# Sixteen products of the identity with itself on TensorE, ahead of the fourth unit of attention

## The chip, the cores and the metric

One Trainium2 chip, one of its cores. The metric is the device time of one execution in microseconds (us), and of several executions the median. TensorE (PE in the rows) multiplies matrices, VectorE (DVE) and ScalarE (ACT) work element by element, GpSimd (POOL) and SyncE (SP) here only fill the identity and start transfers.

## The reference

Attention in blocks of 64 over 576 positions, then two feed-forward layers over the 2304 tokens, all in 32-bit floats. Cut to what matters here:

```python
scores = scale * np.matmul(q, k.transpose(0, 1, 3, 2))          # 4 batches x 8 heads, 576 x 576
scores = np.where(block_i >= block_j, scores, -1000000000.0)
attn = np.exp(scores - np.max(scores, axis=-1, keepdims=True))
attn = attn / (np.sum(attn, axis=-1, keepdims=True) + 1e-09)
x = np.matmul(attn, v)                                           # -> 2304 tokens x 512
h = x @ w_in;  g = softplus(h);  x = g @ w_out                   # 512 -> 2048 -> 512
h = x @ w_in2; e = softmax(h) * h, normalised; out = e @ w_out2  # 512 -> 1024 -> 512
```

## The kernel before

The program is one list of tasks for five engines. Each task has an engine, a planned duration, a rank (lower goes first) and the tasks that it needs. A planner (`Plan.run`) plays the list through with the planned durations and, each time that an engine is free, takes the ready task of lowest rank; what comes out is a fixed order of instructions for each engine. On the chip every engine works through its order and waits at semaphores, so an instruction that isn't ready holds up all behind it.

The start is made of three kinds of work that share the engines. The first 256 positions of each pair of heads are handled by sixteen units `UnitA`: a load of q and k (`qkA`), a score product into a PSUM bank (`mm_qk`: four products, each of which the trace shows as two instructions), on VectorE a mask and two maxima (`mask`, `max`, `scale`), on ScalarE the exponentials (`exp`), on VectorE the division (`norm`), on TensorE six transposes (`tr`), a copy to SBUF (`psA`), the product with v (`pv`), and the result split in two into `xt`. The first four units use the banks `R`, `r`, `acc` and, for the fourth, the two banks `hp0` and `hp1` in which the first feed-forward layer later builds its hidden values. Beside them, `Piece` turns weights that come in by DMA (`raw`) into two parts each, on ScalarE (L273) and VectorE (L276 to L293). `Pair` is the feed-forward layer itself: products `hp<-xt,w`, softplus, and products into `acc`.

The identity matrix `ident`, 128x128, is filled by GpSimd in the first task of all (`open_a`, here the task `t_open`). Transposes use it as one operand. A product of 32-bit floats on TensorE goes in two passes (the two instructions above).

The later stages (the remaining 320 positions, the second feed-forward layer) are not touched by the change.

Of the kernel before, what the change touches and what calls it, by code (L numbers as in the profile page):

```python
# [51 lines left out]
class Plan:  # L52
# [8 lines left out]
    def add(self, eng, dur, rank, fn, deps=(), lat=None):  # L61
        t = _Task()
        t.key = key_of(fn)

        t.alts = dict(eng) if isinstance(eng, dict) else {eng: dur}
        name, i = t.group = self.group
        t.local = rank
        t.rank = rank + RANK[name][0] + RANK[name][1] * i + OFF.get(t.key, 0.0) + OFF.get(t.key + "@" + name, 0.0)
        t.eng, t.fn, t.n, t.done = None if len(t.alts) > 1 else eng, fn, len(self.tasks), False
        t.lat = (self.LAT + (120.0 if eng == "PE" else 0.0)) if lat is None else lat  # L70
        t.users, t.left, t.ready = [], 0, 0.0
        for d in deps:
            if d is not None:
                d.users.append(t)
                t.left += 1
        self.tasks.append(t)
        return t
# [5 lines left out]
    def chain(self, eng, rank, steps, deps):  # L83
        for dur, fn in steps:
            t = self.add(dur if isinstance(dur, dict) else eng, dur, rank, fn, deps)
            deps = [t]
        return t
# [83 lines left out]
def key_of(fn):  # L171
    while isinstance(fn, partial):
        fn = fn.func
    return ".".join(fn.__qualname__.split(".")[-2:])
# [6 lines left out]
def dve_ns(n, per=1.04):  # L181
    return 70.0 + per * n
# [6 lines left out]
def dma_ns(nbytes, n=1):  # L189
    return max(50.0 + nbytes / 360.0, 550.0 * n)  # L190
# [3 lines left out]
def body(ctx: ExitStack, tc: tile.TileContext, qk, qkA, vP, vA, w1, w2, u1, u2, gln, out):  # L194
    nc = tc.nc
    PE, ACT, DVE, POOL, SP = nc.tensor, nc.scalar, nc.vector, nc.gpsimd, nc.sync
    plan = Plan()
    XTB, LAG = 3, 2
    add, chain = plan.add, plan.chain
    DMA_LAT = 1700.0  # L200

    def mm(out, lhsT, rhs, start, stop):
        PE.matmul(out, lhsT, rhs, start=start, stop=stop, skip_group_check=True)  # L203
# [9 lines left out]
    def at_of(lst, i):  # L213
        return lst[i] if 0 <= i < len(lst) else None
# [25 lines left out]
    ident = pw.tile([128, 128], F32, name="ident")  # L240
    gcol = pw.tile([128, 48], F32, name="gcol")[:, 0:8]
    acc = qsh.tile([128, 2, 512], F32, name="acc")
    hps = [qsh.tile([128, 2, CT], F32, name=f"hp{i}") for i in range(2)]
# [3 lines left out]
    class Piece:  # L247
# [3 lines left out]
        def plan(self, prev, rank, get, nr, na, first=(), free=()):  # L251
            oldr, olda = at_of(prev, len(prev) - nr), at_of(prev, len(prev) - na)
            self.get, self.n = get, len(prev)
            dep = ([prev[-1].t_load] if prev else []) + ([oldr.t_bits] if oldr else []) + list(first)
            self.t_load = add("SP", dma_ns(524288), rank, self.load, dep, DMA_LAT)
            t = add("ACT", 570, rank, self.abs, [self.t_load] + ([olda.t_lo] if olda else []))
            self.t_bits = chain("DVE", rank, ((335, self.bits0), (602, self.bits1), (602, self.bits2)), [t])
            if self.g is None:
                self.t_hi = add({"ACT": 520, "DVE": 335}, None, rank, self.do_hi, [self.t_bits] + list(free))
                self.t_lo = add("DVE", 610, rank, self.do_lo, [self.t_hi])  # L260
            else:
                self.t_hi = add("ACT", 520, rank, self.do_hi_g, [self.t_bits] + list(free))
                self.t_lo = add("DVE", 602, rank, self.do_lo_g, [self.t_hi])
            prev.append(self)
# [54 lines left out]
    def xfree(c):  # L319

        return [t for u in pairs if u.c == c - XTB for t in (u.t_a0, u.t_a1)]
# [142 lines left out]
    class UnitA:  # L464
# [6 lines left out]
        def plan(self, prev, rank, opened):  # L471
            n = self.n = len(prev)
            p1, p2 = at_of(prev, n - 1), at_of(prev, n - 2)

            def g(u, *names):
                return [getattr(u, x) for x in names] if u else []


            self.bank = ("R", "r", "acc", "hp")[n] if n < 4 else "r" if n in (8, 9, 10, 11) else ("r", "R")[n % 2]
            free = [u.t_xl for u in prev if u.bank == self.bank][-1:]  # L480
            if n >= 12 and self.bank == "R":
                free += evacs[1]
            self.t_qk = add("SP", dma_ns(262144), rank - 2, self.load_qk, [opened] + g(p1, "t_v") + g(at_of(prev, n - 3), "t_mqk"), DMA_LAT)
            self.t_v = add("SP", dma_ns(131072), rank - 2, self.load_v, [opened, self.t_qk] + g(p2, "t_pv"), DMA_LAT)
            self.t_mqk = add("PE", 760, rank, self.mm_qk, [self.t_qk] + free)
            t = chain("DVE", rank, ((200, self.mask), (330, partial(self.max, 0)), (600, partial(self.max, 1)), (70, self.scale)), [self.t_mqk])
            t = add("ACT", 1580, rank, self.exp, [t] + g(p2, "t_tr"))
            t = chain("DVE", rank, ((72, self.den0), (90, self.den1), (918, self.norm)), [t])
            self.t_tr = add("PE", 650, rank, self.tr, [t])
            self.t_cp = add({"ACT": 708, "DVE": 870}, None, rank, self.copy, [self.t_tr] + g(p1, "t_pv"))  # L490
            self.t_pv = add("PE", 718, rank, self.pv, [self.t_cp, self.t_v])
            self.t_xh = add({"ACT": 264, "DVE": 335}, None, rank, self.x_hi, [self.t_pv] + xfree(self.b))
            self.t_xl = add("DVE", dve_ns(NA), rank, self.x_lo, [self.t_xh])
            xparts.setdefault(self.b, []).append(self.t_xl)
            prev.append(self)
# [229 lines left out]

    NR, NCA = 3, 4
    t_open = add("POOL", 500, 0.0, open_a, ())

    pairs, unitsA, unitsC = [], [], []
    pieces, w1ready, w2ready = [], {}, {}  # L730
# [278 lines left out]
```

## Time and profile before

| | |
|---|---|
| three runs | 818.89, 815.85, 818.53 us; median 818.53 us |
| profiled execution, its own time | 818.25 us |
| span in the profile, first to last instruction | 816.5 us |
| TensorE busy | 790.5 us (97% of the span) |
| VectorE busy | 546.0 us (67%) |
| ScalarE busy | 391.9 us (48%) |
| mean granted TensorE clock | 0.991 |

The time of an execution is 1.75 us more than its span: what lies before the first and after the last instruction. Granted clock 1.00 stands for TensorE's full 2.4 GHz, 0.50 for 1.2 GHz. The busy shares are means over the whole span; the first 60 us look quite different from the rest, and the rows further down show them apart.

### The profile page before, as it was taken

Reading aid. Unit: us, or ns where it says so; the run is one execution under the profiler, and the core shown is the slowest. Engines: PE = TensorE matmul, PEld = TensorE weight load, DVE = VectorE, ACT = ScalarE, POOL = GpSimd, SP = SyncE. Lnnn points to the kernel's source line nnn. Section 1 sums busy time; section 2 is a strip of 40 time slices with the busy share of each in tenths; the row PEclk is TensorE's granted clock in tenths of the full one; section 3 lists DMA queues with packets and bytes.
Section 4 is the critical chain, followed back from the end, with each engine's and each line's share of the span. In section 5 each row is a group of like instructions: output and inputs, shape, how many; then the busy total and the mean of one; then the engine's idle time right before and its main releaser. Section 6 shows DMA issues by size and latency. Waiting matters only on the chain.

```text
span 816.5 us, 14229 instructions
## 1 busy us (share of the span) xinstructions
PE 790.5 (97%) x5656; PEld 684.6 (84%) x5656; DVE 546.0 (67%) x1273; ACT 391.9 (48%) x863; POOL 0.7 (0%) x6
## 2 busy tenths in 40 slices
PE   5689999999999999999999999999999999999998
PEld 3478889998888788888887889999988888888887
DVE  6989999575666665665565652776949576766661
ACT  5566775554555545455554543645623232322232
POOL 0000000000000000000000000000000000000000
PEclk9799999999999999999999999999999999999999
DMA  5636551202121112112211100326301111110001
GB/s 166 214 119 192 175 165 63 92 10 79 49 83 41 42 42 67 41 42 71 61 41 41 58 3 26 105 78 207 117 27 39 51 39 53 39 51 27 26 26 51
DMA packets 31201, 59.63 MB, mean 73 GB/s; under 512 B 2848, under 2 KB 14368, under 8 KB 31136
## 3 DMA queue, kind: packets, MB, share of 16 engines
q1 hardware_dynamic: 31136, 58.74, 22.5%
q8 instruction: 44, 0.72, 0.4%
q14 instruction: 21, 0.17, 0.1%
HBM read 49.29 MB, written 9.44 MB: 72 GB/s over the span
## 4 chain that ended last, share of the span: by engine, by line
PE 80%; DVE 13%; DMA 3%; ACT 2%; issue 2%; SPq 0%; ACTq 0%; DVEq 0%
PE hp L203 19%; PE acc L203 18%; PE op L203 12%; PE h L203 11%; PE S L203 6%; PE O L203 5%; PE T L437 4%; PE tp L905 2%; PE R L203 2%; DVE a L283 2%; DMA raw<-in_w_dram 2%; DVE a L279 1%; DVE t L641 1%; DVE gl L649 1%; PE r L203 1%
## 5 line engine op out<-in xcount | busy, mean ns | idle before, releaser
L203 PE MATMUL hp<-xt,w 128*128 128x256 f32 x1728 | 218.9, 281 | 1.1 <-DVE t L641 1.0
L203 PEld LDWEIGHTS hp<-xt,w 128*128 128x128 f32 x1728 | 205.9, 189 | 5.4 <-issue 3.4
L203 PE MATMUL acc<-gh,w 128*128 128x256 f32 x768 | 150.3, 286 | 0.0
L203 PEld LDWEIGHTS acc<-gh,w 128*128 128x128 f32 x768 | 122.4, 189 | 13.0 <-issue 12.5
L203 PE MATMUL acc<-gl,w 128*128 128x256 f32 x384 | 107.0, 279 | 0.6 <-DVE gl L649 0.6
L203 PE MATMUL op<-w,w2w 128*128 128x512 f32 (+1 forms) x456 | 102.3, 381 | 0.0
L203 PE MATMUL h<-u,w 128*128 128x512 f32 x432 | 100.9, 390 | 0.0
L203 PEld LDWEIGHTS h<-u,w 128*128 128x128 f32 x432 | 80.7, 188 | 16.5
L203 PEld LDWEIGHTS op<-w,w2w 128*128 128x128 f32 x456 | 81.5, 188 | 15.3
L632 ACT ACTIVATE t<-hp 128x512 f32<-128x512 f32 x72 | 42.9, 596 | 79.3 <-PE hp L203 74.5
L209 ACT ACTIVATE ps<-T 128x512 f32<-128x512 f32 (+1 forms) x77 | 42.7, 554 | 75.0 <-PE T L437 60.3
L203 PEld LDWEIGHTS acc<-gl,w 128*128 128x128 f32 x384 | 72.7, 189 | 0.8 <-DVE gl L649 0.8
L641 DVE SCALAR_TENSOR_TENSOR t<-hp,t 128x512 f32<-128x512 f32 x72 | 49.4, 686 | 26.4 <-ACT t L638 26.0
L416 ACT ACTIVATE eC<-S,mC 128x384 f32<-128x384 f32 (+2 forms) x80 | 51.7, 653 | 11.6 <-DVE mC L410 11.5
L406 DVE TENSOR_REDUCE mC<-S 128x2 f32<-128x768 f32 (+2 forms) x48 | 46.9, 976 | 7.9 <-PE S L203 7.2
L203 PE MATMUL S<-qkC 64*128 64x384 f32 (+2 forms) x192 | 51.9, 533 | 0.0
L649 DVE TENSOR_TENSOR gl<-t,gh 128x512 fp32r<-128x512 f32 x72 | 49.6, 689 | 2.8 <-ACT gh L209 1.5
L203 PE MATMUL acc<-gh,w2w 128*128 128x256 f32 x256 | 50.2, 285 | 0.9 <-DVE gh L211 0.7
L857 ACT ACTIVATE e<-h,mx 128x1024 f32<-128x1024 f32 x18 | 20.1, 1116 | 55.1 <-PE tp L905 48.6
L203 PEld LDWEIGHTS acc<-gh,w2w 128*128 128x128 f32 x256 | 40.5, 188 | 6.9 <-issue 5.5
L638 ACT ACTIVATE t<-t 128x512 f32<-128x512 f32 x72 | 45.4, 630 | 2.0
L635 ACT ACTIVATE t<-t 128x512 f32<-128x512 f32 x72 | 45.4, 631 | 1.1
(149 smaller groups left out, 1050.4 us busy)
## 6 DMA issues: line engine op xcount, KB each, us to landing
raw<-in_w_dram SPq DMA_DIRECT2D x32, 512.0 KB, 3.9
qkC<-in_qk_dram SPq DMA_DIRECT2D x16, 480.0 KB, 3.4
raw_u<-in_u_dram SPq DMA_DIRECT2D x11, 512.0 KB, 3.5
v<-in_vP_dram SPq DMA_DIRECT2D x16, 320.0 KB, 3.0
x2s<-stg SPq DMA_DIRECT2D x18, 256.0 KB, 2.2
xr<-x2s SPq DMA_DIRECT2D x18, 256.0 KB, 3.1
qkA<-in_qkA_dram SPq DMA_DIRECT2D x16, 256.0 KB, 3.3
out_dram<-ob SPq DMA_DIRECT2D x15, 256.0 KB, 2.0
```

The source lines that it names most:

```text
L203: PE.matmul(out, lhsT, rhs, start=start, stop=stop, skip_group_check=True)
L209: ACT.activation(out, a, AF.Copy)
L283: DVE.scalar_tensor_tensor(out=self.a, in0=self.raw[:, :, 0], scalar=29, in1=self.a, op0=ALU.logical_shift_right, op1=ALU.bitwise_or)
L406: DVE.tensor_reduce(out=self.m[:, 0:n], in_=self.scores(i), axis=AX.X, op=ALU.max, negate=True)
L416: ACT.activation(state["eC"][i][:, j, :], self.scores(i)[:, j, :], AF.Exp, scale=0.125, bias=m[:, j:j + 1], accum_out=den[:, j:j + 1])
L437: PE.transpose(T[:, 128 * k:128 * k + 128], e[:, 128 * k:128 * k + 128], ident)
L632: ACT.activation(self.t, self.hp, AF.Abs)
L635: ACT.activation(self.t, self.t, AF.Exp, scale=-1.0)
L638: ACT.activation(self.t, self.t, AF.Ln, bias=1.0)
L641: DVE.scalar_tensor_tensor(out=self.t, in0=self.hp, scalar=0.0, in1=self.t, op0=ALU.max, op1=ALU.add)
L649: DVE.tensor_sub(self.gl, self.t, self.gh)
L857: ACT.activation(self.e, self.hh, AF.Exp, bias=self.mx, accum_out=self.ss)
```

## The change

Sixteen tasks are added. Each is one product of the identity with itself, 128x128 by 128x128, written to the bank `hp1`. They need only `t_open`; their rank is 1,000,000 plus what the group adds, so the planner takes one only when no other task of TensorE is ready. The score product of the fourth unit, which takes `hp0` and `hp1`, is made to come after them. Nothing reads what they write.

```diff
@@ UnitA.plan
             if n >= 12 and self.bank == "R":
                 free += evacs[1]
+            if self.bank == "hp":
+                free += idle
@@ body
     t_open = add("POOL", 500, 0.0, open_a, ())
+
+    def idle_product():
+
+        mm(hps[1][:, 0, 0:128], ident, ident, True, True)
+
+
+    idle = [add("PE", 400, 1e6, idle_product, [t_open]) for i in range(16)]
```

On TensorE, at the very start of the program, the order of before is this. `R`, `r` and `acc` are the banks of the first three units; `qkA` is a unit's q and k, `eA_130` and `eA_131` are exponentials of the first two units; x2 means that a row stands for two products.

```order
L203 MATMUL R<-qkA 128x128 x2
L203 MATMUL R<-qkA 128x256 x2
L203 MATMUL r<-qkA 128x128 x2
L203 MATMUL r<-qkA 128x256 x2
L203 MATMUL acc<-qkA 128x128 x2
L203 MATMUL acc<-qkA 128x256 x2
L556 MATMUL R<-ident,eA_130 128x128 x6
L556 MATMUL r<-ident,eA_131 128x128 x6
```

And this is the order of the changed kernel at the same place (its line 558 is line 556 of before).

```order
L203 MATMUL hp_115<-ident 128x128 x7
L203 MATMUL R<-qkA 128x128 x2
L203 MATMUL R<-qkA 128x256 x2
L203 MATMUL hp_115<-ident 128x128
L203 MATMUL r<-qkA 128x128 x2
L203 MATMUL r<-qkA 128x256 x2
L203 MATMUL hp_115<-ident 128x128 x2
L203 MATMUL acc<-qkA 128x128 x2
L203 MATMUL acc<-qkA 128x256 x2
L203 MATMUL hp_115<-ident 128x128 x6
L558 MATMUL R<-ident,eA_130 128x128 x6
L558 MATMUL r<-ident,eA_131 128x128 x6
```

The sixteen products (`hp_115` is `hp1`) stand in four places: seven ahead of the first unit's scores, one and two ahead of the second's and the third's, and six between the third's scores and the first transposes. Behind that TensorE's order is unchanged. The first of the seven waits for GpSimd's identity; the first transpose no longer needs to.

VectorE, ScalarE, SyncE and GpSimd keep their orders word for word, and their waits too. What VectorE does at this start is this: mask, maxima and scaling (L523, L528, L531) of the three units, in turn, then the divisor of the first (L541, L544).

```order
L523 MEMSET R 64x4x64
L528 TENSOR_REDUCE mA<-R 128x2 x2
L523 MEMSET r 64x4x64
L531 TENSOR_SCALAR mA<-mA 128x4
L528 TENSOR_REDUCE mA<-r 128x2 x2
L523 MEMSET acc 64x4x64
L531 TENSOR_SCALAR mA<-mA 128x4
L528 TENSOR_REDUCE mA<-acc 128x2 x2
L541 TENSOR_SCALAR dA<-dA 128x4
```

Nothing moved there.

## Rows read from the trace of the kernel before

**Rows 1.** The page: span, engines' busy time, share and instructions.
```profile
span 816.5 us, 14229 instructions
PE 790.5 (97%) x5656; PEld 684.6 (84%) x5656; DVE 546.0 (67%) x1273; ACT 391.9 (48%) x863; POOL 0.7 (0%) x6
```

**Rows 2.** Windows: from:to, length, busy (instructions) by engine, granted clock, DMA share, GB/s.
```profile
0.00:9.81 9.81, 4.96 (x24) 2.80 (x24) 2.62 (x8) 2.99 (x9) 0.70 (x6) 1.00 0.75 256
9.81:41.40 31.59, 20.45 (x120) 14.87 (x121) 31.25 (x95) 20.59 (x62) 0.00 (x0) 0.84 0.51 166
60.00:140.00 80.00, 76.61 (x651) 72.22 (x651) 77.70 (x172) 54.07 (x115) 0.00 (x0) 1.00 0.47 152
140.00:800.00 660.00, 658.80 (x4656) 569.33 (x4655) 416.82 (x956) 299.38 (x643) 0.00 (x0) 1.00 0.18 55
```

**Rows 3.** Timeline, first 28 us, TensorE: start, length, work [idle before, releaser].
```profile
3.69 1.65 PE L203 MATMUL R<-qkA 64*128 64x128 f32 x8 [3.69 <-DMA qkA<-in_qkA_dram]
5.87 1.65 PE L203 MATMUL r<-qkA 64*128 64x128 f32 x8 [0.53 <-DMA qkA<-in_qkA_dram]
8.02 1.66 PE L203 MATMUL acc<-qkA 64*128 64x128 f32 x8 [0.49 <-DMA qkA<-in_qkA_dram]
...
11.96 1.69 PE L556 MATMUL R<-ident,eA 128*128 128x128 f32 x6 [2.29 <-ACT eA L537]
...
19.73 0.93 PE L203 MATMUL hp<-qkA 64*128 64x128 f32 x8 [0.17 <-DMA qkA<-in_qkA_dram]
...
27.62 1.65 PE L203 MATMUL R<-qkA 64*128 64x128 f32 x8 [3.77 <-DMA qkA<-in_qkA_dram]
```

**Rows 4.** Timeline of the first 10 us and of 41 to 43 us, VectorE.
```profile
5.47 0.27 DVE L523 MEMSET R<- 64x256 f32 x1 [5.47 <-PE R L203]
...
7.66 0.27 DVE L523 MEMSET r<- 64x256 f32 x1 [0.86 <-PE r L203]
...
9.81 0.27 DVE L523 MEMSET acc<- 64x256 f32 x1 [0.82 <-PE acc L203]
...
43.09 0.27 DVE L523 MEMSET r<- 64x256 f32 x1 [1.27 <-PE r L203]
```

**Rows 5.** Timeline of the first 11 us, GpSimd's last fill of the identity, and ScalarE.
```profile
1.00 0.29 POOL masks.py:199 TENSOR_SCALAR_AFFINE_SELECT ident<-ident 128x128 f32<-128x128 f32 x1
...
8.10 0.37 ACT L537 ACTIVATE eA<-R,mA 128x128 f32<-128x128 f32 x1 [6.09 <-DVE mA L531]
...
10.24 0.37 ACT L537 ACTIVATE eA<-r,mA 128x128 f32<-128x128 f32 x1 [0.42 <-DVE mA L531]
```

**Rows 6.** Timeline, TensorE: full 32-bit products (two), and what comes next.
```profile
202.72 1.19 PE L203 MATMUL S<-qkC 128*128 128x512 f32 x4
203.72 1.66 PE L203 MATMUL hp<-xt,w 128*128 128x256 f32 x12
```

**Rows 7.** Windows of one us: granted clock (before DMA share) where it changes.
```profile
28.00:29.00 1.00, 1.00 (x8) 0.55 (x6) 1.00 (x6) 1.00 (x7) 0.00 (x0) 0.50 0.76 311
...
33.00:34.00 1.00, 1.00 (x6) 0.79 (x6) 1.00 (x3) 0.33 (x2) 0.00 (x0) 0.76 0.02 7
...
37.00:38.00 1.00, 1.00 (x5) 1.00 (x6) 1.00 (x6) 0.33 (x1) 0.00 (x0) 0.50 1.02 369
...
40.00:41.00 1.00, 1.00 (x9) 1.00 (x8) 1.00 (x3) 0.24 (x1) 0.00 (x0) 0.84 0.04 16
...
54.00:55.00 1.00, 1.00 (x8) 0.67 (x5) 1.00 (x5) 0.32 (x2) 0.00 (x0) 0.50 0.00 0
...
57.00:58.00 1.00, 1.00 (x8) 0.95 (x7) 0.97 (x3) 0.00 (x0) 0.00 (x0) 0.81 1.10 422
```

**Rows 8.** Timeline, TensorE, 36 to 47 us.
```profile
36.03 0.87 PE L203 MATMUL r<-psA,vA 128*64 128x256 f32 x8 [1.99 <-DVE psA L211]
36.83 2.89 PE L203 MATMUL hp<-xt,w 128*128 128x256 f32 x12
...
43.69 3.01 PE L203 MATMUL hp<-xt,w 128*128 128x256 f32 x24
```

## The prediction

> **What bounds the kernel now.** I read the page first, then the windows, then the timeline of the first 60 us.
>
> The profile's page [rows 1] says that TensorE is busy for 790.5 of 816.5 us, so 26 us are left in which it does nothing, and a change that adds products can only win in those. The windows [rows 2] show where they lie. From 140 us on TensorE is busy for 658.8 of 660 us: nothing waits there, and whatever the earlier part gains or loses is handed on whole to the end. From 60 to 140 us VectorE (77.7 of 80) and TensorE (76.6) are both nearly full. From 9.81 to 41.40 us VectorE is busy for 31.25 of 31.59 us, TensorE for only 20.45: VectorE sets the pace there. Before 9.81 us VectorE works for 2.62 us and otherwise waits for scores. So the kernel's start is bounded by how soon VectorE gets its first three banks of scores.
>
> The timeline shows those waits. The three score products start when their loads land, at 3.69, 5.87 and 8.02 us [rows 3], and take 1.65, 1.65 and 1.66 us. VectorE masks each bank 0.13 us after it is done, at 5.47, 7.66 and 9.81, and was idle for 0.86 and 0.82 us before the second and the third [rows 4]. From the third mask on it has no idle stretch worth naming until 43.09 us, where it waits 1.27 us for a score product.
>
> The reader is to see one more thing in rows 3. The same eight instructions that take 1.65 us at first take 0.93 us at 19.73, and 1.65 us again at 27.62. In that last place the granted clock is 0.50 [rows 7], the lower level of 1.2 GHz. The windows give 1.00 for the first microseconds [rows 2], but the durations contradict it; I go by the durations and take the first three units, and the first transposes (1.69 us at 11.96), to run at the lower level.
>
> **The change, step by step.** It removes nothing and moves nothing on the other four engines. It adds 16 products to TensorE.
>
> *The price of one.* The trace of before has no such product. The nearest row is a 32-bit product with all 128 rows: 512 and 64 columns, 576 in all, start at 202.72 and the next work at 203.72 [rows 6], 1.74 ns a column. 128 columns are then 0.22 us at the full clock and, twice that, 0.44 us at the lower. From below: six transposes of the same size take 1.69 us at the lower level [rows 3], 0.28 us each. I take 0.44, since two passes are what a product makes and a transpose is a single instruction; both ends stay in the range.
>
> *The seven in front.* The identity is done at 1.29 us [rows 5]. From about 1.35 us seven products at 0.44 end at 4.45; at 0.28 they end at 3.3. The first load lands at 3.69, so the first scores are late by 0.76 us, or not at all. Behind them on TensorE's queue are the other two units, and VectorE waits for all three.
>
> *The clock.* The seconds from 28 to 58 us [rows 7] show the granted clock at 0.50 in three stretches and between the levels at their ends: 0.76, 0.84 and 0.81 mean that it rose near 33.5, 40.3 and 57.4 us. In the first two TensorE had gone back to nearly unbroken work at 27.62 [rows 3] and 36.03 [rows 8], 5.9 and 4.3 us earlier. Before 9.81 us, by contrast, work with gaps of half a microsecond, 4.96 us of it from 3.69 on, had not brought the clock up by 11.96. With the products work begins at 1.35 and has no gap until the third load. If it goes as in those two places, the clock is up between 5.6 and 7.3 us.
>
> *The three units then.* First scores 4.45 to about 6.0, one product, second scores from 6.2 to 7.1 (0.93 at the full clock), two products to 7.6, third scores from their landing at 8.02 to 8.95. VectorE: first mask at 6.1 instead of 5.47. It needs 1.33 us for a bank (5.47 to 6.80, which is 7.66 less its idle 0.86), so it is free at 7.4, finds the second bank ready, is free at 8.75, and masks the third at 8.95 + 0.13 = 9.08 instead of 9.81. The gain is 0.73 us. With the clock up only at 7.3 us the second scores end at 7.7, the third run from 8.16 to 9.09 and the mask is at 9.22: a gain of 0.59. A cheaper product changes nothing, since the third load's landing sets it.
>
> *Who else must keep up.* ScalarE begins its first exponentials at 8.10 and its second at 10.24, after an idle 0.42 [rows 5]. With the second scaling ready at about 9.4, it is ScalarE's own first block, 1.72 us from about 8.0, that lets the second begin at 9.7, 0.54 earlier. The second divisor on VectorE waits for neither. The six products behind the third scores end at 8.95 + 6 x 0.22 = 10.3 us; the first transposes, 0.73 earlier, would be at 11.2. The idle 2.29 us there hides them, with 0.9 to spare at the full clock; at the lower one (2.7 us) they would hold the transposes up.
>
> *What of it reaches the end.* VectorE is full from there to 41.40, TensorE or VectorE nearly full to 140, TensorE full after. A shift of 0.73 us passes through. The faster transposes and products between 11 and 17 us are beside VectorE's work and are counted at nothing.
>
> Sum: 818.25 (the profiled execution, 816.5 of span and 1.75 around it; 0.28 below the median of the three runs) - 0.73 = 817.5 us.
>
> By rows 3 the three scores at the lower level have 2.2 us more than at the full one, and all but 0.73 of that lies beside the loads and VectorE's own work. The Trainium skill ("TensorE: Matmul & The Clock Gate", Part 1, "What's actually happening") puts the price of the slow start at under 1% of a typical kernel's span. By that, as an estimate, the sum could be anything down to 810 us; the trace doesn't contradict the page, but bounds the gain far more tightly.
>
> **The rivals.**
> 1. *The clock comes up too late.* For it: before, nearly five microseconds of work by 9.81 us [rows 2] did not lift it. Then all of it runs at the lower level: first scores 4.45 to 6.03, one product, second scores from 6.47, two products, third scores from 8.93 to 10.59, mask at 10.72, 0.91 us later than before. The six products (2.66 us) end at 13.2, 0.3 us after the transposes could start. 818.25 + 0.9 = 819.2, or 819.5 with the transposes. It decides where the third scores end later than 9.68. The Trainium skill says in the same section that the chip's watch on TensorE runs free of the kernel's start, so that one kernel warms up at another instruction from run to run; a single trace can't show that.
> 2. *Nothing reaches the end.* The gain of VectorE is lost at 43.09, where it waits for TensorE, if the stretch at the lower clock there begins at the same time as before: then 818.25. Against it: TensorE's work there follows VectorE's copy, so it starts earlier too.
> 3. *The later slow stretches move as well.* At 37 to 40 us and at 54 to 57 us the granted clock is 0.50 [rows 7], both beside TensorE work that is waited for. Twelve products take 2.89 us in the first, 24 take 3.01 at the full clock [rows 8], 1.4 us too much. Taking as much for the second, both gone gives 817.5 - 2.8 = 814.7; one more gives 818.9. Other gaps decide whether they fall there, and those only shift.
>
> **How the numbers follow.** The forecast has 0.58, rival 1 0.15, rival 2 0.10, rival 3 0.12 with both stretches gone, 0.05 for what I don't see. The three runs of before lie 3 us apart, as much as rival 3, and a stretch that falls otherwise is the likeliest reason I have for it. So the range is 814.9 (nearly both gone) to 819.7 (rival 1 with its transposes). 0.5% is 4.1 us, about what a measurement of this kernel can tell from no change; only rival 3 with the forecast comes near it, at 3.8. Faster 0.05, same 0.93, slower 0.02.
>
> **What would show it.** Right: seven products from 1.35 us at some 0.44 each; the second and third scores at 0.93 us; the mask of `acc` at about 9.1 with VectorE idle for less than 0.4 us before it; the transposes at 11.2, six in about 1 us; VectorE ahead of before by 0.7 us at 40 us. Wrong: the third scores still 1.65 us long, or beginning after 8.6; the first transposes waiting for products; or the same lead at 20 us and none at 60.

## The result and the profile after

The changed kernel takes 821.33 us (median of 6 runs, 818.78 to 825.86), the one before 817.52 us (6 runs, 815.85 to 818.89): ratio 1.0051, 95% interval 1.0028 to 1.0074. Timed again with more runs it was 820.32 against 818.35 us, ratio 1.0027 (1.0012 to 1.0043; below). It is slower, by some 2 to 4 us; 817.5 us and a small gain were forecast. The profiled execution took 820.95 us.

The page after: span, engines, and of the DMA queues the one with the engines' code (packets, MB, share).

```profile
span 819.2 us, 14293 instructions
PE 794.4 (97%) x5688; PEld 687.8 (84%) x5688; DVE 545.9 (67%) x1273; ACT 391.9 (48%) x863; POOL 0.7 (0%) x6
q8 instruction: 45, 0.74, 0.4%
```

Against [rows 1] TensorE has 32 products and 32 weight loads more (a product of 32-bit floats is two of each), 64 instructions, and 3.9 us more of work. The code queue had 44 packets and 0.72 MB before.

The start went nearly as forecast. First TensorE's timeline after, then VectorE's, in the columns of [rows 3] and [rows 4].

```profile
1.35 3.36 PE L203 MATMUL hp<-ident 128*128 128x128 f32 x14 [1.35 <-POOL ident masks.py:199]
4.64 1.38 PE L203 MATMUL R<-qkA 64*128 64x128 f32 x8
5.95 0.49 PE L203 MATMUL hp<-ident 128*128 128x128 f32 x2
6.37 0.93 PE L203 MATMUL r<-qkA 64*128 64x128 f32 x8
7.22 0.71 PE L203 MATMUL hp<-ident 128*128 128x128 f32 x4
7.87 0.93 PE L203 MATMUL acc<-qkA 64*128 64x128 f32 x8
8.72 1.60 PE L203 MATMUL hp<-ident 128*128 128x128 f32 x12
23.05 1.65 PE L203 MATMUL r<-qkA 64*128 64x128 f32 x8 [2.12 <-DMA qkA<-in_qkA_dram]
```

```profile
6.15 0.27 DVE L525 MEMSET R<- 64x256 f32 x1 [6.15 <-PE R L203]
7.52 0.27 DVE L525 MEMSET r<- 64x256 f32 x1
8.92 0.27 DVE L525 MEMSET acc<- 64x256 f32 x1
9.72 1.02 DVE L530 TENSOR_REDUCE mA<-acc 128x2 f32<-128x256 f32 x2 [0.46 <-ACT eA L539]
24.82 0.27 DVE L525 MEMSET r<- 64x256 f32 x1 [0.46 <-PE r L203]
```

The reader is to see the first scores starting at 4.64, behind the seven products, the second and third scores at the full clock's 0.93 us, and the mask of `acc` at 8.92 instead of 9.81. Then the lead of 0.89 us melts. At 9.72 the third unit's maxima have waited 0.46 us for ScalarE: they go into a buffer `mA`, of which the kernel has two, and the first unit's exponentials read the one that is due until 9.69. At 24.82 VectorE has waited another 0.46 us, for the fifth unit's scores, which take 1.65 us. In the trace of before those scores took 0.93 us, and the mask behind them was at 24.88.

```profile
22.93 0.93 PE L203 MATMUL r<-qkA 64*128 64x128 f32 x8 [1.47 <-DVE a L276]
```

Windows of one us (granted clock before DMA share), two of after and then one of before, show why those scores are slow: after, the clock falls near 22.7 us, in a stretch in which TensorE does nothing from 20.9 to 23.05; before, it was up until 26.7 us.

```profile
22.00:23.00 1.00, 0.00 (x0) 0.00 (x0) 1.00 (x5) 0.67 (x2) 0.00 (x0) 0.84 0.49 117
23.00:24.00 1.00, 0.95 (x6) 0.96 (x8) 1.00 (x4) 0.00 (x0) 0.00 (x0) 0.50 0.74 201
```

```profile
26.00:27.00 1.00, 0.00 (x0) 0.00 (x0) 1.00 (x4) 1.00 (x6) 0.00 (x0) 0.83 0.52 117
```

To find the loss I set the start of every VectorE instruction after against the same instruction before. The difference is -0.1 us at 60 and -0.3 at 80 us: no loss yet. It is +1.0 at 84, +1.5 for a moment at 118, +0.7 at 140, then level to 540, and +2.7 from 570 us to the end. The big single step is at 84 us. From the chain of waits (start, length, what), before and then after, the piece that ends there:

```profile
77.43 4.47 DMA raw<-in_w_dram
```

```profile
77.10 5.82 DMA raw<-in_w_dram
```

A load of weights, issued 0.33 us earlier, lands 1.0 us later. The same in ScalarE's timeline, which waits for it, before and after:

```profile
81.98 0.68 ACT L273 ACTIVATE a<-raw 128x512 f32<-128x512 f32 x1 [1.89 <-DMA raw<-in_w_dram]
```

```profile
83.00 0.68 ACT L273 ACTIVATE a<-raw 128x512 f32<-128x512 f32 x1 [3.01 <-DMA raw<-in_w_dram]
```

The records of single DMA packets show what else ran then. Counted from them: ends of the load queue's packets in each half microsecond, and the packet of TensorE's code (16,384 bytes each time) that is nearest, with its start and length.

```
from us         79.0 79.5 80.0 80.5 81.0 81.5 82.0 82.5 83.0 83.5   code packet
before            11   15   40   48   36    2    0    0    6   20   82.59, 1.22 us
before, again     42    8   19   42   49   21    2    0    0    3   82.67, 0.97 us
after              9   41   49   32    5    2    5    4   15   45   79.98, 0.93 us
after, again      48   47    5    1    3    4    4   31   55   54   78.88, 1.46 us
```

Before, a load's packets end in one burst and the code packet comes when they are through. After, the code packet lies in the load, and the last 15 to 20 packets of the load come one by one over about 2 us.

### The profile page after: what moved, and what is told of

It reads as the page before. It is cut to its first block, busy times and chain, and to the rows that moved or that the text cites. A ratio compares the mean times of both kernels' runs of the same rounds, so it can differ in the third digit from the quotient of the medians.

```text
span 819.2 us, 14293 instructions
## 1 busy us (share of the span) xinstructions
PE 794.4 (97%) x5688; PEld 687.8 (84%) x5688; DVE 545.9 (67%) x1273; ACT 391.9 (48%) x863; POOL 0.7 (0%) x6
## 4 chain that ended last, share of the span: by engine, by line
PE 80%; DVE 11%; DMA 4%; ACT 2%; issue 2%; SPq 0%; POOLq 0%; POOL 0%; ACTq 0%; DVEq 0%
PE hp L203 19%; PE acc L203 17%; PE op L203 12%; PE h L203 11%; PE S L203 6%; PE O L203 5%; PE T L437 4%; PE tp L914 2%; PE R L203 2%; DMA raw<-in_w_dram 2%; PE r L203 1%; DVE a L283 1%; DVE a L279 1%; DVE t L643 1%; DVE gl L651 1%
```

## The experiments

Three theories stood against each other. **L**: the weight loads land later, by chance or through the other timing of the start. **C**: TensorE's clock, raised early, falls early, and what that costs is the loss. **K**: TensorE's code is longer and lies elsewhere; after the first four kernels and the packets above this became: code is fetched in blocks while the program runs, and 64 instructions more move every later block to another moment. All ratios are to the kernel before, timed on the same chip among the same runs.

**Both kernels again, word for word.** No edit.

> The kernel before, word for word, timed against itself: it tells what two equal programs differ by here. All theories: ratio 1.000, with an interval that holds 1. Its profile is a second one of before: the landing of the three weight loads that are issued near 77 us and those of the second layer's weights near 540 to 590 us show by how much one program differs from itself there. If 1 is outside the interval, a difference of some 0.5% is no evidence of anything.

Ratio 0.9988 (0.9975 to 1.0000). Its profile has VectorE 1.06 us ahead of the first trace of before at 14 us, without any product: the loads landed sooner, and the clock was up at 7.0 us by itself (and down again at 10.4).

```profile
3.48 1.65 PE L203 MATMUL R<-qkA 64*128 64x128 f32 x8 [3.48 <-DMA qkA<-in_qkA_dram]
5.15 1.65 PE L203 MATMUL r<-qkA 64*128 64x128 f32 x8
6.60 1.01 PE L203 MATMUL acc<-qkA 64*128 64x128 f32 x8
```

By 43 us the lead is gone (+0.2): VectorE waits there 2.51 us for scores, where it waited 1.27 in the first trace. The clock was low without a break from 27.5 to 41.1 us, so the first products of the pairs and what lies about them took longer than in the first trace, which had it up from 33.5 to 36.9 us.

> The changed kernel, word for word. Theory L (loads): the 4 us are not in the first 60 us, where the profile after has no loss, but in weight loads that land later (5.8 instead of 4.5 us near 77 us, and near 540 to 590 us); if that is systematic, ratio 1.004 to 1.006 again and the same places in this profile; if it was the luck of those executions, ratio 0.999 to 1.002 and other places. Theory C (clock): the loss lies where TensorE's clock falls, 23 instead of 27 us; ratio again 1.005, and the profile loses at 20 to 60 us.

Ratio 1.0027 (1.0012 to 1.0043). 1.0 us ahead up to 60 and 1.2 at 80 us, and 0.45 behind at 84: the same place, and this time 1.7 us. Theory C falls, since nothing is lost by 80 us; luck is unlikely, since it comes again.

**The same number of instructions, next to no work.** A product of one column with one column (1x1, called empty below) in place of each full one.

```diff
-        mm(hps[1][:, 0, 0:128], ident, ident, True, True)
+        mm(hps[1][0:1, 0, 0:1], ident[:, 0:1], ident[:, 0:1], True, True)
```

> Sixteen products in the same places, of one column of the identity with itself (1x1 results): the same number of further instructions, next to no work on TensorE. Theory K (code): what costs is that TensorE's code is longer and lies elsewhere; ratio 1.004 to 1.006 as in the changed kernel. Theories L and C: the clock stays low as before and the start is as before; ratio 0.999 to 1.001, and masks of the three banks at 5.5, 7.7 and 9.8 us.

Ratio 1.0019 (1.0002 to 1.0036). The start runs at the lower clock as expected, yet 1.3 us go at 84 us, where ScalarE's wait is 3.13 us. That is for K, though the ratio is below K's 1.004 to 1.006 and its interval reaches close to 1.

**Only the seven products in front** (28 of the 64 further instructions).

```diff
-        mm(hps[1][:, 0, 0:128], ident, ident, True, True)
+        if i < 7:
+            mm(hps[1][:, 0, 0:128], ident, ident, True, True)
```

> Only the seven products in front of the first scores; the other nine are left out. Theory C: the clock rises at nearly the same point (5 to 8 us), so that the start is like the changed kernel's and the loss the same, ratio 1.004 to 1.006. If the nine others matter (the clock falls earlier, or the six hold up something), ratio 0.998 to 1.002. Mask of acc at about 9 us in both cases.

Ratio 1.0000 (0.9987 to 1.0014). The clock rises at 5 us as in the changed kernel, ScalarE waits 1.78 us, nothing is lost at 84. C had said 1.004 or more here.

**The code alone, moved by a whole, a quarter, a half and three quarters of a block.** 64 instructions are a quarter of a block of 256: a packet of 16,384 bytes at 64 bytes each; 14,229 instructions in all, of which TensorE's 5656 products and 5656 weight loads make the 44 packets. The edit is shown for sixteen; of 48 and 64 a part lies ahead of the fifth unit's scores.

```diff
+            for _ in range({5: 16}.get(self.n, 0)):
+                mm(self.banks[0][0:1, 0:1], ident[:, 0:1], ident[:, 0:1], True, True)
             self.m, self.den = self.t([128, 2, 2], "mA"), self.t([128, 2, 2], "dA")
```

> The kernel before with 64 products of 1x1, 28 ahead of the fifth and 36 ahead of the sixth unit's scores, a whole block of code more and no other change. Theory K: ratio 0.999 to 1.001. If the number of further instructions costs by itself: 1.003 or more, since it is four times that of the changed kernel.

> The kernel before with sixteen products of 1x1 ahead of the sixth unit's scores, where TensorE is idle for 3.8 us: nothing is changed at the start, only the code behind is moved by a quarter of a block, as in the changed kernel. Theory K: ratio 1.001 to 1.004, the weight load near 77 us in some 5.5 to 6 us, ScalarE waiting 3 us or more for it, and the loss of 1 us or more at 84 us. If the loss needs the sixteen full products or their place in the first 10 us: 0.999 to 1.001 and a wait of 2 us.

> The same with 32 products, half a block. Theory K: a block falls elsewhere again, near 77 us or less than 2 us after: other loads are hit, the ratio lies anywhere from 0.998 to 1.005, but the weight load near 77 us is not the one that is late, or by less. If only the number of instructions counts: between the ratio with 16 and that with 64.

> The kernel before with 48 products of 1x1, 16 ahead of the fifth and 32 ahead of the sixth unit's scores: three quarters of a block. Theory K: a fourth phase of the code, with no reason to be like the others: anywhere from 0.998 to 1.004; what decides is whether a block is loaded while a weight load is under way that ScalarE waits for, between 77 and 82 us above all. Any theory without code: 1.000.

**The changed kernel, filled up to a whole and to half a block** in the same way, with 48 and sixteen empty products.

> The changed kernel with 48 products of 1x1 more, 20 ahead of the fifth and 28 ahead of the sixth unit's scores, in their own banks, where TensorE is idle for 2 us each. Theory K: TensorE's code is loaded in blocks of 16 KB while the program runs (44 packets, 0.72 MB before, 45 and 0.74 MB after); a product is four instructions, sixteen are a quarter of a block, so that all later blocks are loaded at other moments, and one then falls into the weight load that is issued near 77 us. With 64 products more than before a whole block is added, and the later blocks fall where they fell before: ratio 0.997 to 1.000, the weight load near 77 us in about 4.5 us and not in 5.8. If the cost is of the sixteen full products (clock, start): 1.002 to 1.004, as in the changed kernel.

> The changed kernel with sixteen products of 1x1 more, ahead of the sixth unit's scores: 32 products more than before, half a block of code. Theory K: the same code phase as the kernel before with 32 products of 1x1, so the same ratio, 0.998 to 1.001, and not 1.003; ScalarE's wait for the weight load near 82 us about 2 us and not 3. If the sixteen full products cost something by themselves: 1.002 or more, as in the changed kernel.

All in one table: products more than before, what part of a block they move the code by, the ratio, ScalarE's wait for the weight load near 82 us, and what VectorE loses against the first trace of before between 80 and 84 us. The last two columns are from the records of loads and packets: how long that load took from its issue to its landing, and how long after its issue (before it, with a minus) the code packet nearest to it started.

| kernel | products | block | ratio (95%) | wait | lost | load | packet |
|---|---|---|---|---|---|---|---|
| before, again | 0 | 0 | 0.9988 (0.9975-1.0000) | 1.99 | 0.1 | 4.58 | 4.90 |
| seven in front | 7 | 7/64 | 1.0000 (0.9987-1.0014) | 1.78 | -0.1 | 4.33 | 4.01 |
| changed, first result | 16 | 1/4 | 1.0051 (1.0028-1.0074) | 3.01 | 1.35 | 5.82 | 2.88 |
| changed, again | 16 | 1/4 | 1.0027 (1.0012-1.0043) | 3.62 | 1.7 | 6.14 | 2.67 |
| sixteen of 1x1, same places | 16 | 1/4 | 1.0019 (1.0002-1.0036) | 3.13 | 1.3 | 5.76 | 2.82 |
| sixteen of 1x1, at 23 us | 16 | 1/4 | 1.0032 (1.0017-1.0047) | 2.79 | 0.8 | 5.28 | 1.97 |
| 32 of 1x1 | 32 | 1/2 | 0.9994 (0.9977-1.0011) | 1.86 | -0.1 | 4.39 | -2.57 |
| changed, and 16 of 1x1 | 32 | 1/2 | 1.0003 (0.9989-1.0018) | 1.67 | -0.2 | 4.23 | -2.64 |
| 48 of 1x1 | 48 | 3/4 | 1.0005 (0.9989-1.0021) | 1.89 | -0.2 | 4.05 | -6.72 |
| 64 of 1x1 | 64 | 1 | 1.0000 (0.9987-1.0013) | 1.97 | 0.1 | 4.56 | 5.29 |
| changed, and 48 of 1x1 | 64 | 1 | 1.0002 (0.9990-1.0014) | 2.14 | 0.2 | 4.68 | 5.08 |

Theory K holds in every line. What was added doesn't matter, nor where, as far as was tried: sixteen empty products at 23 us cost about as much as the sixteen full ones (0.8 us at 84, a little less than K had put there), and the changed kernel with 48 empty products on top shows no cost. Of the steps tried only a quarter of a block does it; at three quarters nothing is lost at 84 us, but the interval leaves room for 0.2%. The packets show the mechanism itself: in the four profiles with a quarter of a block a code packet starts 2.0 to 2.9 us into the load, in the others it starts outside it or in its last 0.3 us. Theory L falls with the same profiles: those that lose stand from 1.2 us ahead to 1.2 behind at 80 us, those that don't from 1.1 ahead to 0.9 behind, so the timing of the start doesn't decide it. The load in question, in the chain of waits of sixteen empty products at 23 us, and of the changed kernel filled to a whole block:

```profile
78.61 5.28 DMA raw<-in_w_dram
```

```profile
78.30 4.68 DMA raw<-in_w_dram
```

**Filling the later gaps.** Full products of the identity in gaps of TensorE at 15, 21, 25 and 34 us (1.3 to 3.8 us long in the first trace of before), with empty ones up to 64 in all; once with the sixteen of the change (shown; `fill` takes the number of full and of empty ones) and once without.

```diff
+            fill(self.banks[0], {4: (5, 2), 5: (8, 9)}.get(self.n))
             self.m, self.den = self.t([128, 2, 2], "mA"), self.t([128, 2, 2], "dA")
...
+            fill(hps[1][:, 0] if self.n == 1 else acc[:, 0], {1: (8, 4), 4: (8, 4)}.get(self.n))
             self.o = self.banks[0][:, 0:NA]
```

> The changed kernel with 29 full products of the identity more in four places where TensorE is idle for about 2 us (eight ahead of the second unit's product with v, five and eight ahead of the fifth and sixth unit's scores, eight ahead of the fifth unit's product with v), and 19 of 1x1, 64 in all, so that the code stands as before. Theory: VectorE's lead at 10 us is lost by 25 to 43 us, because TensorE's clock falls in these gaps and the scores of the fifth and sixth unit and the first pairs then run at the lower level. With the gaps filled the clock stays up to 51 us, the scores at 23 and 27 us take 0.93 us, the first twelve products of the pairs 1.5 us and not 2.9: ahead of before by 0.7 to 2 us at 60 us, ratio 0.9975 to 0.999. Rival: the lead is lost to the loads of these units, whatever the clock: no lead at 45 us, ratio 1.000.

> The same without the sixteen products of the change: only the four later gaps are filled (29 full products, 35 of 1x1, 64 in all, the code stands as before). If what counts is the clock from 23 to 51 us: as e_warm, a lead of 0.7 to 1.5 us at 60 us. If the start is what counts: no lead at 20 us and none later, ratio 1.000.

With the sixteen: 816.34 us, ratio 0.9982 (0.9964 to 1.0000). Without: 816.53 us, ratio 0.9979 (0.9963 to 0.9995). At 60 us VectorE is 1.9 and 1.4 us ahead of the first trace of before; that is one profile each, and without any filling it stood between 1.2 us ahead and 1.3 behind. The clock wasn't up all the way (it was low from 28 to 32 us), but the pairs' first products come at the full one, in the kernel with the sixteen:

```profile
35.12 0.87 PE L203 MATMUL r<-psA,vA 128*64 128x256 f32 x8 [0.24 <-DVE psA L211]
35.92 1.68 PE L203 MATMUL hp<-xt,w 128*128 128x256 f32 x12
```

Twelve products in 1.68 us, and 1.65 in the other, against 2.89 [rows 8] and 2.4 to 2.9 in all profiles without the filling. This is what the forecast had hoped for, got in another place: where TensorE, not VectorE, is waited for. Of the two versions only the one without the change's sixteen products has an interval clear of 1.

## Why the prediction was wrong

**The price of a product** was right: 3.29 us from the first to the first scores is 0.47 each, 0.44 were forecast. **The clock** came up where it was put (5.6 to 7.3 us) in the profile after: at 5.6 us, so that the first scores took 1.38 us, between its two levels, and the next two 0.93. That it did so in this profile is in part luck: in the four others with the sixteen products it rose at 4.4, 4.6, 6.8 and 7.2 us. **The six products** were hidden. **The masks** were at 6.15, 7.52 and 8.92, forecast 6.1, 7.4 and 9.08.

**The first step that failed is the 0.73 us itself**. It was measured against one trace whose third load landed late, at 8.02. In the eight traces with no full product ahead of the third scores (the two of before, the four with only empty ones behind, that with sixteen empty ones in front, and the later gaps filled) the mask of `acc` is at 8.3 to 9.8 us, mean 8.92. In the five with the sixteen it is at 8.4 to 9.6, mean 8.96 (at 9.5 and 9.6 in the two where the clock rose last). Each group scatters by some 0.5 us, so a small gain can't be excluded, but 0.73 us isn't there in the mean. Where the loads land sooner, the first scores lose by the products in front what the others gain by the clock. "A cheaper product changes nothing, since the third load's landing sets it" doesn't carry over to the other traces: in seven of those eight the third scores began at 6.60 to 7.62.

**The second is "a shift of 0.73 us passes through".** The step on ScalarE left out that VectorE's third maxima wait for the first unit's exponentials. Those ended at 9.69 us against 9.82 before, and that, not the mask, sets what VectorE can gain: of 0.89 us at the mask 0.46 were left at 14 us. At that place the eight traces are 0.67 us ahead of the first trace of before in the mean, the five with the sixteen products 0.47. For the rest rival 2 had the mechanism, not the place: the lead was gone at 25 us in the profile after, and in the second of before at 43, each time at scores or first products that ran at the lower clock or waited for their load. The prediction's own sign of being wrong, a lead at 20 us and none at 60, came true (0.46 and 0.08). The later experiments bear that out: with the clock up for most of that stretch, 1.4 to 1.9 us of lead stand at 60 us, and the medians, 816.34 and 816.53 against 818.23 us, are lower by as much.

**The third, which decided the sign, is a term that the sum did not have.** That the change "moves nothing on the other four engines" left out that TensorE's code is itself loaded by DMA. Sixteen products are a quarter of a block, so every later block is fetched at another moment, and one falls into a weight load that ScalarE waits for, then VectorE, then TensorE: 0.8 to 1.7 us at 84 us. That this is the cause of the loss at 84 us is shown by the two sets of experiments that move the code without the work and put it back with the work. The Trainium skill ("Runtime: NRT & Kernel Launch", "Instruction fetch mechanics") says that code comes in blocks of 16 KiB, 256 instructions, over a DMA queue of the engine's own, and that crossing into the next is mostly hidden. The first half agrees with the 44 and 45 packets here. The second agrees for TensorE, which was busy for 658.8 of 660 us from 140 us on [rows 2] while 37 such packets came; what the quarter of a block cost was not at TensorE but at the load beside it.

It is not the whole of the loss. From 80 us to the end the four profiles with a quarter of a block (after, again, and both with sixteen empty ones) lose 3.0, 2.9, 1.6 and 0.7 us against the first of before, 2.1 in the mean; the nine others between -0.4 and +0.8, in the mean 0.07. About 1.3 of the 2.1 is at 84 us. Where the rest goes differs between profiles of the same kernel (after: 1.9 between 540 and 570 us, where the changed kernel again loses nothing) and stays open. That the code packet and the late packets share one DMA engine is argued from the one-by-one tail; the records don't name the engine.

**The range** was too narrow as well: its upper end was rival 1, and nothing in it stood for a loss behind the first 60 us. It was built on three runs 3 us apart; 35 runs of before reach from 813.82 to 821.35 us.

## What to carry to other kernels

An instruction that costs an engine nothing still moves all of its code behind it; where loads set the pace, compare two versions whose counts of that engine's instructions differ by whole blocks (here 256), or fill up with empty instructions, before believing 0.3%. A wait read in one trace (here scores that began at 8.02 us, and at 6.60 in the next) is a sample: take it from two traces before building a gain on it. A clock that is up is worth having where TensorE itself is waited for; ahead of VectorE, which set the pace, it bought nothing that could be measured here (1.0002 with the code at its old place). And when one wait is shortened, look for the next engine that the same step waits for: here ScalarE stood right behind TensorE.

## What the runs showed of the hardware

A 16 KB packet of code that started 2.0 to 2.9 us into a 512 KB load took 0.9 to 1.5 us, and the load took 5.3 to 6.1 us, against 4.0 to 4.7 in the ten profiles in which no packet started there. A packet in the first 0.6 us of the next load went with 3.9 us instead of 3.3 to 3.5 in three profiles of four; the ratios of the kernels with and without it are alike. And TensorE's clock came up at 7.0 us in one execution of the kernel before and at 16.4 us in another. In the five profiles with the sixteen products, where TensorE works from 1.35 us on, it came up between 4.4 and 7.2 us. So the granted clock of the first microseconds differs from run to run with the same program.
